# Matmuls without readers at three waits of TensorE in a kernel of attention and two layers

## The chip, the cores and the metric

The kernel runs on one core of one Trainium2 chip. The metric is the device time of one execution in microseconds (us), as a median of several executions. The engines are named as in the profile: PE is TensorE's matmul, PEld its weight load, DVE is VectorE, ACT ScalarE, POOL GpSimd, SP SyncE, which issues most DMAs.

## The reference

Attention over B=2 batches, H=8 heads, S=576 positions and head size 64 keeps the 32 largest scores of each row, takes the softmax over them and multiplies by the values. The result, 1152 tokens of 512, goes through two layers:

```python
scores = scale * np.matmul(q, k.transpose(0, 1, 3, 2))
kth = np.partition(scores, -32, axis=-1)[..., -32:-31]
attn = softmax(np.where(scores >= kth, scores, -1e9))
x = (attn @ v)                                    # to 1152 x 512
h = x @ w_in;  g = np.maximum(h, 0) + alpha * np.minimum(h, 0)
x = g @ w_out                                     # moe1: 512 -> 2048 -> 512
out = (x @ w_a) * (x @ w_b) @ w_out2              # moe2: 512 -> 1536 -> 512
```

## The kernel before

The tokens are cut into six groups of 128, 128, 256, 256, 256 and 128 (M1), numbered 0 to 5 in the code. Each group passes three kinds of work: attention, the first layer (moe1) and the second (moe2). Attention goes in 72 tiles of 128 query rows by 576 keys, numbered in the order in which they run. Tiles 16 to 31 belong to group 2, the third; tiles 32 to 35 are the first of group 3 and take the last 64 rows of two heads at a time; from tile 36 on the tiles belong to batch 1.

One tile goes through these steps. front() (L439 to L442): PE computes the scores into `ps`, a PSUM tile of two banks whose tag "S" has a single buffer, 288 columns in each bank, and ACT copies them to `s`. middle(): DVE takes the 8 largest four times (MAX8 on L450 and L459, MATCH_REPLACE8 on L457 between them); meanwhile ACT writes the exp of `s` into `ep` (L463), which takes the same single buffer of tag "S" as `ps`; DVE selects by the 32nd value and sums (L466), so it frees the buffer; POOL divides by the sum (L473). back(): in batch 0 PE transposes the tile (L500, L502) and ACT copies it out (L501, L503); in batch 1 the tile is split into two fp16 parts and transposed by a DMA that SP issues (L495). av(): PE multiplies by the values (L534 in batch 0 with 20 matmuls, L529 in batch 1 with 27 and one more), ACT (L542) and DVE (L543) write the two fp16 parts of the result, `xT`. The scores of the next tile are asked for while the present one is scanned.

moe1 of a group: for each of 16 blocks of features, l1 computes `h` on PE in 12 matmuls (L614, 256 columns in groups 2 to 4), ACT scales it to `r` (L649), DVE forms `gt` (L650), ACT and POOL split it in two parts `gp` (L604, L605); l2 accumulates `y` three blocks later (L626, 512 columns). finish() scales `y` by a power of two from its squares (ACT L684, DVE L114 to L116), splits it (ACT L694, DVE L695), transposes it on PE into `tp` (L699, PSUM tag "T" with two buffers, which the transposes of attention and av's result share), and ACT copies it to `xT` (L700). moe2 then computes `ha` and `hb` (L614, 12 matmuls each), ACT L753 and DVE L754 multiply them, and `o` accumulates (L626). Beside all this the weights are converted in the background (ACT L253 and L264, ACT L254 and L265, POOL L255 and L266), w2 through DRAM.

The order of the stages is ORDER: the two layers of groups 0 to 3 in turn, then moe1 of 4 and 5, then moe2 of 4 and 5. Three tracks (attention, conversion, layers) are interleaved by a planner's clock when the program is written; the framework then schedules the instructions of all engines by its own timeline, with priorities, and so sets the order on each engine. Each engine runs its queue in that order.

## Time and profile before

| | us |
|---|---|
| median of 3 runs | 723.14 |
| lowest, highest | 721.69, 1243.16 |
| the profiled execution | 723.9 |
| its span, first to last instruction | 722.0 |
| mean granted clock of TensorE, as a share of full speed | 0.942 |
| busy PE | 620.3 (86%) |
| busy DVE | 576.0 (80%) |
| busy ACT | 472.5 (65%) |
| busy POOL | 429.5 (59%) |

The prediction's sum is made against the profiled execution, and is then moved by its difference from the median. The busy shares are means over very different stretches; the rows below are taken from single ones.

### The profile page before, as it was taken

How to read it: one execution, taken by the hardware profiler on the slowest of the kernel's cores; microseconds unless marked ns; L12 is line 12 of the kernel's file. 1: busy time of each engine (PE TensorE's matmuls, PEld its weight loads, DVE VectorE, ACT ScalarE, POOL GpSimd, SP SyncE). 2: the span in 40 equal slices, each digit the busy share in tenths (PEclk: the TensorE clock that was granted, in tenths of full speed). 3: DMA queues.
4: the chain of work that ended last, by engine and by line, in shares of the span. 5: the costliest groups of instructions: out<-in, count | busy, mean ns of one | idle time of the engine just before them, and what ended most of it. 6: DMA issues, size and time to landing. Idle time of an engine off the chain costs nothing.

```text
span 722.0 us, 14587 instructions
## 1 busy us (share of the span) xinstructions
PE 620.3 (86%) x4950; PEld 459.4 (64%) x4950; DVE 576.0 (80%) x1462; ACT 472.5 (65%) x967; POOL 429.5 (59%) x608
## 2 busy tenths in 40 slices
PE   2555758899989898879977999998899989899997
PEld 1334546678666676656735777765677767677775
DVE  4999899779999998799788889999899989322121
ACT  5957988797699896789778544556455545543232
POOL 5856788888456675679787655555355545321111
PEclk9998678999999998979996999999799999999999
DMA  6966998995440041222547544422355531102233
GB/s 183 336 201 197 308 310 272 311 340 154 137 117 25 15 113 37 78 75 80 151 138 202 155 106 109 108 56 58 47 104 125 102 64 34 34 2 59 63 128 103
DMA packets 98490, 94.55 MB, mean 131 GB/s; under 512 B 50416, under 2 KB 72688, under 8 KB 98416
## 3 DMA queue, kind: packets, MB, share of 16 engines
q1 hardware_dynamic: 97104, 91.26, 44.5%
q10 hardware_dynamic: 1312, 2.36, 1.1%
q8 instruction: 39, 0.64, 0.4%
q14 instruction: 35, 0.29, 0.1%
HBM read 74.33 MB, written 8.65 MB: 115 GB/s over the span
## 4 chain that ended last, share of the span: by engine, by line
PE 43%; DVE 22%; ACT 9%; DMA 8%; issue 6%; POOL 4%; SPq 1%; POOLq 0%; DVEq 0%; ACTq 0%
DVE wk L457 6%; PE h L614 6%; DVE m L459 6%; PE y L626 5%; PE hb L614 5%; PE ha L614 5%; PE o L626 5%; DVE e L466 3%; PE ps L439 3%; DMA pt<-e 3%; PE hb L618 2%; PE ha L618 2%; DMA w2s<-w_st 2%; DVE m L450 2%; PE o L534 2%
## 5 line engine op out<-in xcount | busy, mean ns | idle before, releaser
L459 DVE MAX8 m<-wk 128x8 f32<-128x576 f32 x216 | 163.0, 754 | 2.5
L605 POOL TENSOR_TENSOR gp<-gt,gp 128x256 f16<-128x256 f32 (+1 forms) x112 | 68.3, 612 | 119.0 <-ACT gp L604 108.4
L457 DVE MATCH_REPLACE8 wk<-m,wk 128x576 f32<-128x576 f32 x144 | 106.8, 742 | 0.0
L614 PE MATMUL h<-xT,wi_sb 128*128 128x256 f16 (+1 forms) x960 | 98.3, 251 | 2.1 <-DVE gp_n L663 0.7
L614 PEld LDWEIGHTS <-wi_sb 128*128 128x128 f16 x960 | 79.1, 98 | 23.7 <-issue 7.3
L604 ACT ACTIVATE gp<-gt 128x256 f16<-128x256 f32 (+1 forms) x112 | 43.3, 387 | 68.0 <-DVE gt L754 44.7
L626 PE MATMUL y<-wo_sb,gp 128*128 128x512 f16 x336 | 84.9, 385 | 3.1 <-ACT gp L604 2.0
L626 PEld LDWEIGHTS <-gp 128*128 128x128 f16 x588 | 54.8, 98 | 51.0 <-ACT gp L604 3.8
L439 PE MATMUL ps<-ks,qh 128*128 128x288 f32 x160 | 49.9, 395 | 40.5 <-DVE e L466 31.4
L473 POOL TENSOR_SCALAR e<-e,sm 128x576 f32<-128x576 f32 x72 | 55.2, 767 | 37.7 <-DVE sm L471 36.6
L450 DVE MAX8 m<-s 128x8 f32<-128x576 f32 x72 | 54.2, 753 | 26.3 <-ACT s L442 25.9
L754 DVE SCALAR_TENSOR_TENSOR gt<-hb,wb_inv,r 128x256 f32<-128x256 f32 (+1 forms) x48 | 21.4, 446 | 60.6 <-PE hb L614 60.3
L614 PE MATMUL ha<-xT,wa_sb 128*128 128x256 f16 (+1 forms) x576 | 66.3, 265 | 1.5 <-ACT xT L700 1.3
L614 PE MATMUL hb<-xT,wb_sb 128*128 128x256 f16 (+1 forms) x576 | 63.9, 260 | 0.7 <-DVE gt L754 0.7
L626 PE MATMUL o<-w2s,gp 128*128 128x512 f16 x252 | 63.8, 379 | 0.4 <-ACT gp L604 0.2
L439 PEld LDWEIGHTS ps<-ks,qh 128*128 128x128 f32 x160 | 29.7, 217 | 53.8 <-DVE e L466 28.6
L614 PEld LDWEIGHTS <-wa_sb 128*128 128x128 f16 x576 | 51.6, 100 | 15.8 <-issue 1.9
L466 DVE SCALAR_TENSOR_TENSOR e<-s,m,ep 128x576 f32<-128x576 f32 x72 | 58.1, 806 | 3.0 <-PE t L502 0.7
L442 ACT ACTIVATE s<-ps 128x576 f32<-128x576 f32 x72 | 46.6, 647 | 15.4 <-PE ps L439 14.9
L614 PEld LDWEIGHTS <-wb_sb 128*128 128x128 f16 x576 | 50.7, 98 | 7.7 <-issue 0.7
L195 ACT ACTIVATE rlo<-raw 128x512 int16<-128x512 uint32 x68 | 54.2, 797 | 2.0 <-DMA raw<-in_wi_dram 1.7
L463 ACT ACTIVATE ep<-s,nb 128x576 f32<-128x576 f32 x72 | 54.0, 750 | 1.8 <-DVE e L466 0.6
(204 smaller groups left out, 1435.1 us busy)
## 6 DMA issues: line engine op xcount, KB each, us to landing
w2s<-w_pr SPq DMA_DIRECT2D x48, 256.0 KB, 2.8
w2s<-w_st SPq DMA_DIRECT2D x36, 256.0 KB, 2.8
raw<-in_wi_dram SPq DMA_DIRECT2D x16, 512.0 KB, 6.9
raw<-in_wo_dram SPq DMA_DIRECT2D x16, 512.0 KB, 6.8
raw<-in_wa_dram SPq DMA_DIRECT2D x12, 512.0 KB, 5.4
raw<-in_wb_dram SPq DMA_DIRECT2D x12, 512.0 KB, 5.0
raw<-in_w_dram SPq DMA_DIRECT2D x12, 512.0 KB, 5.0
kr<-in_kT_dram SPq DMA_DIRECT2D x32, 144.0 KB, 2.9
```

Of the source, the lines that this page charges most:

```text
L195: nc.scalar.activation(r.bitcast(I16).rearrange("p (n t) -> p n t", t=2)[:, :, 0], lo, AF.Copy, scale=2.0 ** -29)
L439: nc.tensor.matmul(ps[:, f, 0:HALF], q[:, h % 2, :], ks[h][:, f * HALF:(f + 1) * HALF], start=i == 0, stop=i == len(mm) - 1)
L442: nc.scalar.activation(s.rearrange("p (a n) -> p a n", a=2), ps[:, :, 0:HALF], AF.Copy)
L450: nc.vector.max(m8[:, 0:8], s)
L457: nc.vector.match_replace(out=wk, in_to_replace=m8[:, 8 * r - 8:8 * r], in_values=src, imm_value=NEG)
L459: nc.vector.max(m8[:, 8 * r:8 * r + 8], wk)
L463: nc.scalar.activation(ep, w2(s), AF.Exp, bias=nb, scale=0.125)
L466: nc.vector.scalar_tensor_tensor(w2(e), w2(s), m8[:, 31:32], ep, op0=ALU.is_ge, op1=ALU.mult, accum_out=sm[:, 0:1])
L473: nc.gpsimd.tensor_scalar(e, e, sm[:, 1:2], 1.0, op0=ALU.mult, op1=ALU.mult)
L605: nc.gpsimd.tensor_sub(l[:, 0:n], t[:, 0:n], h[:, 0:n])
L614: nc.tensor.matmul(dst[:, 0:n], w[a][:, c * P:(c + 1) * P], x[:, b, c, 0:n], start=k == 0, stop=k == 11)
L626: nc.tensor.matmul(dst, act[b][:, s], w[a], start=i == 0 and k == 0, stop=i == last and k == 2)
```

## The change

The tiles of attention get their number as `i`. Two tables say where matmuls are added whose results nobody reads:

- WARM_S in front(): for tiles 31, 32 and 33, after ACT's copy of the scores, 14 matmuls of 224 columns into the columns 288 to 511 of the two banks of `ps`, from operands that the scores used.
- WARM in l1: for groups 2 and 3, after the last of the 16 blocks, 16 and 8 matmuls of 256 columns into the second half of `h`.
- WARM in finish(): for groups 2 and 3, before the transposes of token tile 0 and 1, 8 and 6 matmuls of 512 columns into `tp`, which the transposes then write over.

```diff
--- before.py
+++ after.py
@@ -65,6 +65,8 @@
 HPY = 0
 HPM = 100
 SB = 3
+WARM = {2: (16, 8, 6), 3: (8, 8, 6)}
+WARM_S = {31: 14, 32: 14, 33: 14}
 KBACK = 2
 KFRONT = 2
 SHIFT_ATT = 4.0
@@ -392,6 +394,8 @@
                         tiles.append(dict(g=g, b=b, t=t if kind == "T" else 4, hp=hp, hs=hs, n=n, col=cols_of[unit[0]], slot=slot,
                                           wide=len(unit) * P, pts=pts_of, lift=b == 1, last=slot == len(unit) - 1 and i == len(heads) - 1))
         gsize.append(col)
+    for i, tl in enumerate(tiles):
+        tl["i"] = i
 
     def fetch(tl):
         b, t, hp = tl["b"], tl["t"], tl["hp"]
@@ -440,6 +444,8 @@
                                  start=i == 0, stop=i == len(mm) - 1)
         s = sp.tile([P, S], F32, tag="s", name="s", bufs=SB)
         nc.scalar.activation(s.rearrange("p (a n) -> p a n", a=2), ps[:, :, 0:HALF], AF.Copy)
+        for i in range(WARM_S.get(tl["i"], 0)):
+            nc.tensor.matmul(ps[:, i % 2, HALF:512], qh[:, tl["hs"][0] % 2, :], ks[tl["hs"][0]][:, 0:512 - HALF], start=True, stop=True)
         return s
 
     def middle(tl, s):
@@ -649,6 +655,10 @@
                     nc.scalar.activation(r1[:, 0:n], h[:, 0:n], AF.Copy, scale=pre_sig[:, fc:fc + 1])
                     nc.vector.scalar_tensor_tensor(gt[:, 0:n], h[:, 0:n], pre_alp[:, fc:fc + 1], r1[:, 0:n], op0=ALU.mult, op1=ALU.max)
                     gts[fc] = act_split(gt, n)
+                if fc == NF1 - 1 and g in WARM:
+                    for i in range(WARM[g][0]):
+                        nc.tensor.matmul(h[:, 256:256 + n], halves("wi", fc)[0][:, 0:P], xT[:, 0, 0, 0:n], start=True, stop=True)
+                if s2:
                     return
                 r1, r2 = (sized("r1", 2, n, s2), sized("r2", 2, n, s2))
                 nc.scalar.activation(r1[:, 0:n], h[:, 0:n], AF.Relu, scale=pos[:, fc // 2:fc // 2 + 1] if s1 else 2.0)
@@ -693,7 +703,11 @@
                 yh, yl = yb[:, 0:DM], yb[:, DM:2 * DM]
                 nc.scalar.activation(yh, ys[t], AF.Copy, scale=sq[:, 1:2])
                 nc.vector.scalar_tensor_tensor(yl, ys[t], sq[:, 1:2], yh, op0=ALU.mult, op1=ALU.subtract)
-                tp = psum("tp", "T").bitcast(F16).rearrange("p (a c n) -> p a c n", a=2, c=4)
+                tp = psum("tp", "T")
+                if g in WARM:
+                    for i in range(WARM[g][1 + min(t, 1)]):
+                        nc.tensor.matmul(tp, gts[NF1 - 1][0][:, t * P:(t + 1) * P], halves("wo", NF1 - 1)[0], start=True, stop=True)
+                tp = tp.bitcast(F16).rearrange("p (a c n) -> p a c n", a=2, c=4)
                 for i, y in enumerate((yh, yl)):
                     for c in range(4):
                         nc.tensor.transpose(tp[:, i, c, :], y[:, c * P:(c + 1) * P], ident16)
```

The numbers of lines grow by 2 to 14 with the change (L439 becomes L443, L529 L535, L534 L540, L543 L549, L626 L632, L699 L713). PE gets 94 matmuls and 52 weight loads more; the other engines have the same instructions as before in another order.

PE at the end of group 2, before. The lines L500 and L502 are transposes of attention tiles, L439 scores (ks_116 is of tile 32, ks_149 of tile 33), L534 the product with the values, L629 moe2 of group 1:

```order
L629 MATMUL o_3083<-w2s,gp_n 128x512 x2
L500 MATMUL t_3755<-ident,e 128x128 x4
L502 MATMUL t_3756<-ident,e 128x128
L439 MATMUL ps<-ks_116,qh_3615 128x288 x2
L439 MATMUL ps<-ks_116,ql_3616 128x288 x2
L500 MATMUL t_3803<-ident,e 128x128 x4
L502 MATMUL t_3804<-ident,e 128x128
L439 MATMUL ps<-ks_149,qh_3693 128x288 x2
L534 MATMUL o<-pt,v_3629 64x256 x10
```

The same place after the change; L448 are the added matmuls of front(), 14 of them for each of the three tiles (qh_3447 is of tile 31):

```order
L448 MATMUL ps<-ks_422,qh_3447 128x224 x9
L635 MATMUL o_3083<-w2s,gp_n 128x512
L448 MATMUL ps<-ks_422,qh_3447 128x224 x2
L506 MATMUL t_3755<-ident,e 128x128 x4
L508 MATMUL t_3756<-ident,e 128x128
L443 MATMUL ps<-ks_116,qh_3615 128x288 x2
L443 MATMUL ps<-ks_116,ql_3616 128x288 x2
L506 MATMUL t_3817<-ident,e 128x128 x4
L508 MATMUL t_3818<-ident,e 128x128
L448 MATMUL ps<-ks_116,qh_3615 128x224 x14
L443 MATMUL ps<-ks_149,qh_3693 128x288 x2
L540 MATMUL o<-pt,v_3629 64x256 x10
```

The set of tile 31 stands among the last matmuls of `o`, ahead of the transposes; the set of tile 32 stands behind the next transposes and ahead of the scores of tile 33.

PE at the change from moe1 to moe2 in group 2, before. y_3997 and y_3998 are the two token tiles of `y`, ks_4632 belongs to tile 42, vp_2913 and vp_3493 are values, and `tp` the transposes of finish(). Repeated rows are left out:

```order
L439 MATMUL ps<-ks_4632,qh_4644 128x288 x2
L439 MATMUL ps<-ks_4632,ql_4645 128x288 x2
L439 MATMUL ps<-ks_4638,qh_4644 128x288 x2
L439 MATMUL ps<-ks_4638,ql_4645 128x288 x2
L626 LDWEIGHTS gp
L529 LDWEIGHTS vp_2913
L529 MATMUL o<-pt,vp_2913 64x128
L699 LDWEIGHTS yb
L699 MATMUL tp<-ident_72,yb 128x128
```

The same place after; L660 are the added matmuls of l1 (16), L709 those of finish() (8 here). Tile 42's keys are now ks_4674, and `y` is y_4039 and y_4040:

```order
L660 MATMUL h<-xT_2844,wi_sb 128x256
L632 MATMUL y_4039<-wo_sb,gp 128x512
L709 LDWEIGHTS gp
L709 MATMUL tp<-wo_sb,gp 128x512
L535 LDWEIGHTS vp_2913
L535 MATMUL o<-pt,vp_2913 64x128
L632 MATMUL y_4040<-wo_sb,gp 128x512
L443 MATMUL ps<-ks_4674,qh_4686 128x288 x2
L443 MATMUL ps<-ks_4674,ql_4687 128x288 x2
L443 MATMUL ps<-ks_4680,qh_4686 128x288 x2
L535 MATMUL o<-pt,vp_3493 64x64
```

The scores of tile 42 stood ahead of the last `y` and of the product with vp_2913; now they stand behind both, and two sets of added matmuls stand ahead.

DVE at the same place, before; m_5130 are the maxima of tile 42, m_4974 those of tile 41, L543 the second part of the product with vp_2913:

```order
L457 MATCH_REPLACE wk<-m_4974,wk 128x576
L450 MAX m_5130<-s 128x8
L114 TENSOR_SCALAR e_4948<-ysq 128x1
L115 TENSOR_SCALAR ysq<-e_4948 128x1
L114 TENSOR_SCALAR e_5061<-ysq 128x1
L459 MAX m_4974<-wk 128x8
L543 SCALAR_TENSOR_TENSOR xT_3972<-o,xT_3972 128x128
L457 MATCH_REPLACE wk<-m_5130,s 128x576
```

DVE there after; m_5202 are the maxima of tile 42 now, m_5040 those of tile 41, L549 the product's second part, L705 the split of `y`:

```order
L463 MATCH_REPLACE wk<-m_5040,wk 128x576
L549 SCALAR_TENSOR_TENSOR xT_4014<-o,xT_4014 128x128
L116 TENSOR_SCALAR e_5006<-ysq 128x1
L465 MAX m_5040<-wk 128x8
L117 TENSOR_SCALAR ysq<-e_5006 128x1
L116 TENSOR_SCALAR e_5127<-ysq 128x1
L807 TENSOR_SCALAR u<-ysq 128x1
L456 MAX m_5202<-s 128x8
L705 SCALAR_TENSOR_TENSOR yb<-y_4039,ysq,yb 128x512
```

The product's second part stood behind the first scan of tile 42 and the last of tile 41; now it stands ahead of both.

## Rows read from the trace of the kernel before

**Rows 1.** The page's part 2: the span in 40 slices, in tenths.

```profile
DVE  4999899779999998799788889999899989322121
...
PEclk9998678999999998979996999999799999999999
```

**Rows 2.** Stretches: length, busy PE, PEld, DVE, ACT, POOL (count), granted clock, DMA share, GB/s.

```profile
307.30:317.60 10.30, 7.31 (x31) 5.04 (x33) 10.13 (x26) 7.96 (x14) 9.02 (x13) 0.51 0.23 66
375.80:382.30 6.50, 5.07 (x16) 2.79 (x15) 5.63 (x14) 2.71 (x6) 6.36 (x14) 0.50 0.62 151
386.00:396.20 10.20, 7.13 (x62) 5.56 (x63) 8.51 (x21) 9.47 (x18) 8.41 (x11) 0.50 0.89 230
505.30:515.70 10.40, 7.65 (x54) 6.11 (x54) 9.22 (x25) 4.94 (x8) 3.09 (x5) 0.51 0.22 41
420.00:500.00 80.00, 80.00 (x646) 56.90 (x643) 75.33 (x179) 42.74 (x88) 42.71 (x70) 1.00 0.39 89
...
623.00:722.00 99.00, 93.64 (x940) 70.63 (x934) 21.22 (x53) 33.74 (x88) 20.02 (x40) 0.99 0.21 65
```

**Rows 3.** The chain of waits that ends last: start, length, what.

```profile
283.02 2.31 PE o L534 x20
...
322.52 1.33 PE ps L439 x8
...
379.05 2.26 PE ps L439 x8
...
619.10 3.18 DMA pt<-e
622.33 0.94 PE o L529 x27
...
671.40 1.29 PE o L626 x6
672.70 1.31 PE ha L614 x12
```

**Rows 4.** Timeline, all engines, 300 to 322 us; idle time before, and releaser, in brackets.

```profile
304.50 0.76 DVE L450 MAX8 m<-s 128x8 f32<-128x576 f32 x1 [1.08 <-ACT s L442]
...
304.90 0.66 PE L500 MATMUL t<-ident,e 128*128 128x128 f32 x4 [2.33 <-POOL e L473]
...
305.34 0.73 ACT L463 ACTIVATE ep<-s,nb 128x576 f32<-128x576 f32 x1
...
306.91 0.81 DVE L466 SCALAR_TENSOR_TENSOR e<-s,m,ep 128x576 f32<-128x576 f32 x1
...
307.79 0.85 PE L439 MATMUL ps<-ks,qh 128*128 128x288 f32 x2 [2.12 <-DVE e L466]
...
313.91 4.20 PE L534 MATMUL o<-pt,v 128*64 128x256 f32 x20 [2.35 <-ACT pt L501]
...
320.12 0.76 DVE L450 MAX8 m<-s 128x8 f32<-128x576 f32 x1 [0.93 <-ACT s L442]
```

**Rows 5.** Timeline, all engines, 372 to 396 us.

```profile
373.80 0.60 PE L626 MATMUL y<-wo_sb,gp 128*128 128x512 f16 x2 [2.02 <-ACT gp L604]
...
382.03 0.76 DVE L450 MAX8 m<-s 128x8 f32<-128x576 f32 x1 [0.74 <-ACT s L442]
...
382.77 0.97 PE L529 MATMUL o<-pt,vp 128*64 128x128 f16 x27
...
393.40 2.72 PE L614 MATMUL ha<-xT,wa_sb 128*128 128x256 f16 x12 [0.18 <-ACT xT L700]
...
395.21 0.76 DVE L450 MAX8 m<-s 128x8 f32<-128x576 f32 x1 [1.65 <-ACT s L442]
```

**Rows 6.** Timeline, all engines, 503 to 520 us.

```profile
506.55 3.15 PE L529 MATMUL o<-pt,vp 128*64 128x256 f16 x27 [1.58 <-DMA pt<-e]
...
512.75 2.72 PE L614 MATMUL ha<-xT,wa_sb 128*128 128x256 f16 x12 [1.11 <-ACT xT L700]
...
517.05 0.48 DVE L754 SCALAR_TENSOR_TENSOR gt<-hb,wb_inv,r 128x256 f32<-128x256 f32 x1 [1.64 <-PE hb L614]
```

## The prediction

> **What bounds the kernel now.** I read the two lines of the page's 40 slices first [rows 1]. A slice is 18 us. The granted clock of TensorE drops early on (slices 4 to 7), which the change doesn't touch, and then to 7, 6 and 7 in slices 18, 22 and 29, which are the places of the change. VectorE (DVE) is at 7 tenths or more in each slice until the 34th, and at 3 or less behind it. The busy time by stretch then says what the drops are [rows 2]. In four stretches the granted clock is 0.50 or 0.51, which is the lower of the engine's two levels, 1.2 GHz. TensorE (PE) worked 7.31 + 5.07 + 7.13 + 7.65 = 27.2 us in them, and at 2.4 GHz it would have needed half, so 13.6 us is the most that the clock could give back there. Between 420 and 500 us PE is busy in all 80.00 us and DVE in 75.33, so there the two are close to each other as bounds, with 4.67 us of idle DVE.
>
> The chain of waits [rows 3] gives the end: the last attention tile's transpose by DMA (619.10, 3.18 us), its product with the values at 622.33, and behind it only layer work. That tail is PE's: 93.64 of 99.00 us at a clock of 0.99 [rows 2]. The changed order has as many PE rows behind that last product as the old one, so a gain counts only if it brings the last attention tile forward. Attention goes through DVE, which takes its scans strictly in its own order. So I price the change by the DVE idle time that it removes or adds, and treat PE time as the bound only in a rival.
>
> The three places are seen in the timelines. At the third group's tiles [rows 4], PE stands idle 2.33 us before the transposes at 304.90 and 2.12 us before the scores at 307.79, and from there the clock is low. At the first change of layers [rows 5], it idles 2.02 us before the y matmuls at 373.80, then works at the low clock. At the second [rows 6], the product at 506.55 waits 1.58 us for a DMA and is followed by the hidden-layer matmuls ha at the low clock, 2.72 us for twelve.
>
> **The change, part by part.** It removes no instruction. It adds 94 matmuls without readers: 42 of 224 columns in front(), 24 of 256 columns in l1, 28 of 512 columns in finish. The other engines get no work, but the scheduler orders all engines anew.
>
> *Price of the added matmuls.* Eight score matmuls of 288 columns take 1.33 us at the high clock and 2.26 at the low one [rows 3]. Scaled to 224 columns that is 0.129 and 0.22 each, so a set of 14 is an estimated 1.8 us (3.1 if cold). Twelve matmuls of 256 columns take 1.31 us and six of 512 take 1.29 [rows 3], so 0.109 and 0.215 each. In all 42 x 0.129 + 24 x 0.109 + 28 x 0.215 = 14.0 us on PE. The idle PE time within the four cold stretches alone is 37.4 - 27.2 = 10.2 us [rows 2], and more lies just ahead of each, so I cost these matmuls nothing as work. They cost where somebody waits behind them.
>
> *Place A, tiles 31 to 33.* The scores' PSUM slot has one buffer, and the exp output ep takes the same slot next, so the exp waits for the added matmuls. For tile 31 they stand ahead of the DVE gap of 1.08 us at 304.50 [rows 4]; a set of 1.8 us costs between 0 and 0.7, and I take 0. For tile 32 they stand behind the transposes that wait for GpSimd (304.90, 0.66 us long), so they run from about 305.6 to 307.4. The exp that began at 305.34 and took 0.73 then ends near 308.1, and the DVE select that began at 306.91 moves by 1.2 us. For tile 33 I expect no further delay. Against that, the scores at 307.79 should be warm and 0.9 us shorter (2.26 - 1.33), and the product of twenty at 313.91 should take 2.31 us as at 283.02 [rows 3] instead of 4.20. DVE's only idle time behind these is 0.93 us at 320.12 [rows 4], so no more than that comes back. Sum: +1.2 - 0.9 = +0.3, with ends at -0.9 and +3.2 (the set for tile 32 cold, 1.3 more, tile 31's 0.7, and nothing given back).
>
> The Trainium skill has a rule that bears on this place: the page "PSUM — Partial Sum Buffer", section "PSUM bank collisions raise a hardware error", says that two engines must be kept apart by bank, even where their columns are disjoint. By that rule "free columns" are not free: the added matmuls need the copy out of both banks to be over and hold the next user back, which makes place A +0.3; if columns were independent the exp could start as before and A would be -0.9, giving 719.3. The order shows the wait; no run here shows a collision.
>
> *Place B, first change of layers.* The added matmuls wait here for the last activation of l1 and for a slot. The order moves two other things. The scores of one tile now stand behind the product with vp_2913 on PE, and on DVE the xT row of that product stands ahead of a tile's last scans. Before, the product ran at 382.77 and took 0.97 us [rows 5]; with the copy by ScalarE behind it, xT can run near 383.9. DVE arrives there near 381.3 (382.03 less its gap of 0.74). So it waits 2.6 instead of 0.74 us, +1.8. The scores warm give back 0.9 us of the gap of 1.65 at 395.21. Net +0.9, with ends at -2.4 (both gaps gone, no new one) and +5.0 (one transpose of 3.18 more). ha at 393.40 would shrink from 2.72 to 1.31 [rows 3, 5], but that is PE time, which counts in the next term.
>
> *The stretch from 400 to 500.* PE arrives up to 1.4 us earlier by ha and about as much by hb, and DVE has 4.67 us to fill [rows 2]. The order also puts the score matmuls of most later tiles before some us of layer work that they followed. Ends: 0 and -4.7. Just ahead of it the chain runs through DMAs, not PE, so I take a third, -1.5.
>
> *Place C, second change of layers.* The product at 506.55 would halve from 3.15 us, ha and hb too. DVE was idle 1.18 us within the stretch [rows 2] and until 517.05 after it, 1.35 more. All of that should go: about -2.4. The cover is the 1.58 us of DMA wait ahead of the product; the 8 matmuls in h and 8 + 6 in tp are 0.9 + 3.0 us, which delay y, whose readers have time until the transposes after the product. Without cover +1.5 instead. Ends: -2.5 and +1.5.
>
> **Sum.** +0.3 + 0.9 - 1.5 - 2.4 = -2.7 us. The profiled execution took 723.9 us (span 722.0), 0.8 over the median of 723.14. So 721.2 in that execution's terms, and about 720.5 as a median. The ends add up to -10.5 and +9.7, so 713 to 733 if all fell on one side.
>
> **Rivals.**
> *PE bounds throughout.* For it: 80.00 of 80.00 us busy, and a PE queue in which every score stands behind layer work. Then all 27.2 us of cold work count half, -13.6, and the time is 709.5. Against it: in the stretch at 307 DVE is busy 10.13 of 10.30 us while PE has 2.99 idle [rows 2], so there at least the clock is not what ends the stretch.
> The Trainium skill's page "TensorE: Matmul & The Clock Gate", Part 1, says that the ramp costs under 1% of a typical kernel's span; by that no more than 7.2 us could come back, and this rival would end at 716 instead. The trace does not agree with it as a bound: half of 27.2 us is 1.9% of 722.0, since the clock falls more than once.
>
> *Slower: DVE is held by what now stands ahead of it.* The mechanism is place B's and A's: DVE's queue is in order, and the moved xT row and the exps make it wait for a PE queue with cold added matmuls and a DMA transpose in it. If the clock is low when the added sets run, each of the three exps waits 3.1 us, 9.3, and if the transpose comes one later, 3.18 us are added: 12.5 us in all, and the time is 735.6. Half of it is 729. It decides if the added sets run after the fall of the clock, not before. For it: the set for tile 32 stands behind a wait of 2.33 us [rows 4]. Against it: the transposes that end that wait still run at the high clock, four in 0.66 us.
>
> *The change doesn't do what it says.* The added matmuls wait themselves: for ScalarE's copy, for DVE's gt, for a slot in the tag T. If the idle time before them is what lowers the clock, it falls all the same. Then no cold work gets faster, place A and B cost about 2 to 3 us, and some of it is absorbed: 724.5. For it: the gap of 2.02 us at 373.80 [rows 5] stands before the first added matmul of place B can run.
>
> **How the numbers follow.** The forecast gets 0.50; with the distances of its terms from their ends put together as a root of squares (4.7 down, 6.5 up) its own range is 716 to 727. PE as the bound 0.14, DVE held 0.17, no effect on the clock 0.19. The likeliest case gives 720.5. The range goes from 710 to 731: it leaves out the lower half of the PE case and the upper half of the DVE case, and some of each case's own spread, about 0.18. A change of 2%, 14.5 us, is about what a measurement of this kernel can tell from none. Faster than 708.7 needs more than the whole PE case: 0.07. Slower than 737.6 needs the DVE case in full and something more: 0.05. The rest, 0.88, is within 2%.
>
> **What would show it.** Right, if in the changed kernel's profile the granted clock stays near 1.0 through the stretches at 307, 376, 386 and 505, the product of twenty near 314 takes 2.3 us, ha after each change of layers takes 1.3, and the last attention product comes 2 to 4 us before 622.33, with the tail still 99 us. Place A is right if DVE's select of tile 32 waits for its exp, about 1.2 us. Place B is right if the xT row after the product with vp_2913 shows a DVE wait of more than 2 us. The forecast is wrong if the last attention product moves by over 8 us in either direction: forward, if PE was the bound from 400 on; back, if DVE's waits for scores, exps or xT have grown. It is wrong in its ground if the clock still falls at these places, or if the time changes in the tail, which should not move.

## The result, and the profile after

The changed kernel takes 731.52 us (median of four, 727.5 to 733.8); the kernel before took 722.99 beside it. The ratio is 1.0121, with a 95% interval from 1.0083 to 1.0159: slower by 8.5 us, just outside the range of 710 to 731. A second set of nine executions gave 730.27 and 1.0082 [1.0052, 1.0113].

The page's slices, to be read against [rows 1]:

```profile
DVE  4899899789899995888888689999999999222121
...
PEclk9976669999999998989998999999999999999999
```

The clock in slices 18, 22 and 29 reads 8, 8 and 9 now, where it read 7, 6 and 7. The mean clock of these slices rises, as the change meant it to, and the kernel is slower all the same. Its profiled execution took 731.0 us, its span 729.2, with a mean granted clock of 0.94, as before. The stretches of the kernel after say where the clock went (columns as in [rows 2]):

```profile
303.50:312.40 8.90, 3.74 (x28) 3.30 (x28) 6.77 (x16) 6.17 (x12) 5.78 (x9) 0.88 0.22 58
312.40:318.00 5.60, 5.60 (x29) 5.29 (x29) 3.10 (x8) 4.49 (x7) 4.86 (x8) 0.59 0.15 38
...
391.00:402.00 11.00, 7.29 (x62) 4.57 (x63) 10.76 (x28) 9.13 (x17) 8.34 (x13) 0.69 0.85 182
...
512.00:530.00 18.00, 15.31 (x113) 11.35 (x111) 16.99 (x42) 9.73 (x18) 8.41 (x14) 0.91 0.28 45
```

The low stretch has moved and not vanished: it lies at 312 to 318 us now (0.59) and again at 391 to 402 (0.69). At group 3's change of layers (512 to 530) it is nearly gone, 0.91 over 18 us against the 0.51 of [rows 2] over 10.4 us.

**How two profiles are compared here.** All engines' orders are the same in all kernels until tile 28, yet DVE's select of that tile starts between 273.2 and 282.4 us in the profiles; the spread is 1.8 us at the first tile's select and 9.0 at tile 16's, and no run shows its cause. So each select's start is taken from that of tile 28 in the same profile, and compared with the same difference in the kernel before. For tile 32 in the changed kernel: (319.19 - 277.18) - (314.79 - 279.21) = +6.4 us. Tiles are counted from 0. The rows of the kernel before that this needs, and tile 30's:

```profile
279.21 0.81 DVE L466 SCALAR_TENSOR_TENSOR e<-s,m,ep 128x576 f32<-128x576 f32 x1
...
297.36 0.63 ACT L442 ACTIVATE s<-ps 128x576 f32<-128x576 f32 x1
...
298.93 0.73 ACT L463 ACTIVATE ep<-s,nb 128x576 f32<-128x576 f32 x1
...
300.28 0.80 DVE L466 SCALAR_TENSOR_TENSOR e<-s,m,ep 128x576 f32<-128x576 f32 x1
...
301.01 0.60 ACT L796 ACTIVATE ob<-o 128x512 f32<-128x512 f32 x1 [0.37 <-PE o L629]
...
314.79 0.80 DVE L466 SCALAR_TENSOR_TENSOR e<-s,m,ep 128x576 f32<-128x576 f32 x1
```

The scores of tile 31 are copied by 297.99, tile 30's exp, which takes the slot next, starts at 298.93, and the copy of the layer's output (ob) comes behind it on ScalarE. Place A in the changed kernel, timeline of PE, DVE and ACT together:

```profile
277.18 0.81 DVE L472 SCALAR_TENSOR_TENSOR e<-s,m,ep 128x576 f32<-128x576 f32 x1
...
295.96 0.65 ACT L446 ACTIVATE s<-ps 128x576 f32<-128x576 f32 x1 [0.25 <-PE ps L443]
...
297.66 1.24 PE L448 MATMUL ps<-ks,qh 128*128 128x224 f32 x9
...
300.29 0.89 PE L448 MATMUL ps<-ks,qh 128*128 128x224 f32 x3
...
300.89 0.60 ACT L810 ACTIVATE ob<-o 128x512 f32<-128x512 f32 x1 [2.15 <-PE o L635]
...
302.71 0.73 ACT L469 ACTIVATE ep<-s,nb 128x576 f32<-128x576 f32 x1
...
303.55 0.81 DVE L472 SCALAR_TENSOR_TENSOR e<-s,m,ep 128x576 f32<-128x576 f32 x1 [0.44 <-ACT ep L469]
...
306.60 0.76 DVE L456 MAX8 m<-s 128x8 f32<-128x576 f32 x1 [1.84 <-ACT s L446]
...
311.43 0.80 DVE L472 SCALAR_TENSOR_TENSOR e<-s,m,ep 128x576 f32<-128x576 f32 x1
...
312.39 0.82 PE L443 MATMUL ps<-ks,qh 128*128 128x288 f32 x2 [4.02 <-DVE e L472]
...
317.96 2.38 PE L540 MATMUL o<-pt,v 128*64 128x256 f32 x20
...
319.19 0.82 DVE L472 SCALAR_TENSOR_TENSOR e<-s,m,ep 128x576 f32<-128x576 f32 x1 [0.39 <-issue]
```

The set of tile 31 waits for the copy that ends at 296.61, starts at 297.66 behind layer matmuls, and ends at 301.18, because the order has cut it in three with `o` matmuls between: 3.5 us instead of 1.8. Then ScalarE does the output copy, which waited 2.15 us for these `o` matmuls, a conversion and the next queries, and only then the exp, at 302.71. A set holds back the exp of the tile before: the prediction names the exp by the tile of the set, here it is named by its own. DVE selects at 303.55. From the end of the copy to the exp it was 0.94 us before and is 6.1 now. Counted from tile 28's select, the exp starts 5.8 us later than before; the set's end, ahead of which it could not start, accounts for 4.3 of them, and what ScalarE does in between for the last 1.5. PE then stands idle 4.02 us before the scores at 312.39, the clock falls there, and the scores run cold again.

Place B and what follows it:

```profile
383.86 0.97 PE L535 MATMUL o<-pt,vp 128*64 128x128 f16 x27
...
385.25 0.28 DVE L549 SCALAR_TENSOR_TENSOR xT<-o,xT 128x128 f16<-128x128 f32 x1
...
390.92 0.47 PE L535 MATMUL o<-pt,vp 128*64 128x64 f16 x17 [4.06 <-DMA pt<-e]
...
401.69 1.47 PE L620 MATMUL ha<-xT,wa_sb 128*128 128x256 f16 x12 [0.72 <-ACT xT L714]
...
410.81 0.61 PE L443 MATMUL ps<-ks,qh 128*128 128x288 f32 x2
...
411.53 0.43 PE L443 MATMUL ps<-ks,qh 128*128 128x288 f32 x2
...
416.48 0.48 DVE L768 SCALAR_TENSOR_TENSOR gt<-hb,wb_inv,r 128x256 f32<-128x256 f32 x1 [2.61 <-PE hb L620]
...
418.17 0.53 PE L443 MATMUL ps<-ks,ql 128*128 128x288 f32 x2
...
418.75 0.23 DVE L549 SCALAR_TENSOR_TENSOR xT<-o,xT 128x64 f16<-128x64 f32 x1 [1.79 <-ACT xT L548]
...
420.20 0.81 DVE L472 SCALAR_TENSOR_TENSOR e<-s,m,ep 128x576 f32<-128x576 f32 x1
```

The eight scores of tile 45 are cut in two by the order: six at 410.81 to 412.0, the last two at 418.17, with 6 us of layer work between. DVE waits 2.61 and 1.79 us behind that in its queue, and the select of tile 44 slips to 420.20. The product with vp_2913 (383.86, 0.97 us) doesn't wait, and its xT row at 385.25 has no idle time before it; the one that waits 4.06 us for its DMA is the next, with vp_3493. The first ha of moe2, at 401.69, takes 1.47 us here; in a second profile of the same kernel (e10) it takes 2.72. Place C, and the begin of the tail (PE alone):

```profile
510.46 1.69 PE L535 MATMUL o<-pt,vp 128*64 128x256 f16 x27
...
519.41 1.47 PE L620 MATMUL ha<-xT,wa_sb 128*128 128x256 f16 x12 [0.42 <-ACT xT L714]
...
628.18 0.40 PE L713 MATMUL tp<-ident,yb 128*128 128x128 f16 x4 [0.60 <-ACT yb L704]
...
631.19 2.72 PE L620 MATMUL h<-xT,wi_sb 128*128 128x128 f16 x24 [0.85 <-DVE gt L656]
```

The product of 27 takes 1.69 us instead of the 3.15 of [rows 6], ha 1.47 instead of 2.72. In the tail PE waits 0.60 and 0.85 us and runs 24 short matmuls at the low clock, 2.72 us. In the second profile (e10) PE waits 0.85 us there too, but the same 24 run at the high clock:

```profile
630.43 1.50 PE L620 MATMUL h<-xT,wi_sb 128*128 128x128 f16 x24 [0.85 <-DVE gt L656]
```

### The profile page after: what moved, and what is told of

Read it like the earlier page. It is cut to its first block, busy times and chain, and to the rows that moved or that the text cites. A ratio compares the mean times of both kernels' runs of the same rounds, so it can differ in the third digit from the quotient of the medians.

```text
span 729.2 us, 14780 instructions
## 1 busy us (share of the span) xinstructions
PE 630.7 (86%) x5044; PEld 467.5 (64%) x5044; DVE 571.1 (78%) x1462; ACT 470.4 (65%) x967; POOL 430.7 (59%) x608
## 5 line engine op out<-in xcount | busy, mean ns | idle before, releaser
L620 PE MATMUL h<-xT,wi_sb 128*128 128x256 f16 (+1 forms) x960 | 102.1, 257 | 2.3 <-DVE gt L656 1.1
L620 PEld LDWEIGHTS <-wi_sb 128*128 128x128 f16 x960 | 81.3, 100 | 27.1 <-issue 10.0
L443 PE MATMUL ps<-ks,qh 128*128 128x288 f32 x160 | 50.0, 394 | 43.4 <-DVE e L472 34.1
L632 PE MATMUL y<-wo_sb,gp 128*128 128x512 f16 x336 | 85.1, 382 | 0.1
L632 PEld LDWEIGHTS <-gp 128*128 128x128 f16 x588 | 55.3, 98 | 45.6 <-issue 1.5
L443 PEld LDWEIGHTS ps<-ks,qh 128*128 128x128 f32 x160 | 29.6, 212 | 55.9 <-DVE e L472 23.4
L632 PE MATMUL o<-w2s,gp 128*128 128x512 f16 x252 | 64.6, 379 | 0.9 <-DMA w2s<-w_pr 0.5
L620 PE MATMUL ha<-xT,wa_sb 128*128 128x256 f16 (+1 forms) x576 | 63.8, 259 | 1.1 <-ACT xT L714 1.1
L463 DVE MATCH_REPLACE8 wk<-m,s 128x576 f32<-128x576 f32 x72 | 53.4, 742 | 0.0
```

The costliest lines, as they stand in the source:

```text
L443: nc.tensor.matmul(ps[:, f, 0:HALF], q[:, h % 2, :], ks[h][:, f * HALF:(f + 1) * HALF], start=i == 0, stop=i == len(mm) - 1)
L463: nc.vector.match_replace(out=wk, in_to_replace=m8[:, 8 * r - 8:8 * r], in_values=src, imm_value=NEG)
L620: nc.tensor.matmul(dst[:, 0:n], w[a][:, c * P:(c + 1) * P], x[:, b, c, 0:n], start=k == 0, stop=k == 11)
L632: nc.tensor.matmul(dst, act[b][:, s], w[a], start=i == 0 and k == 0, stop=i == last and k == 2)
```

## The experiments

All times are medians beside executions of the kernel before on the same chip, with the ratio and its interval. The table gives the shift of DVE's select (us, later is +) as worked out above, and in the last column that of the end of the span.

| kernel | 30 | 32 | 43 | 44 | 49 | 57 | 58 | 61 | 71 | end |
|---|---|---|---|---|---|---|---|---|---|---|
| changed kernel | +5.3 | +6.4 | +4.6 | +9.7 | +6.0 | +6.1 | +4.8 | +7.3 | +5.9 | +9.2 |
| e10, the same again | +3.9 | +4.6 | +4.2 | +9.5 | +5.9 | +5.9 | +3.9 | +6.7 | +4.5 | +6.1 |
| e1, front() alone | +3.9 | +4.8 | +5.2 | +8.9 | +5.1 | +7.1 | +7.0 | +7.9 | +10.7 | +11.3 |
| e2, layers alone | +0.4 | +0.3 | -0.4 | +7.6 | +2.5 | +3.4 | +1.4 | +2.4 | +4.2 | +4.8 |
| e11, the same again | +0.7 | +0.8 | +2.1 | +9.8 | +4.7 | +5.6 | +3.6 | +4.6 | +6.9 | +7.5 |
| e3, one each | +0.2 | -2.5 | +0.3 | +3.7 | -0.4 | -0.3 | -0.3 | +0.6 | +4.0 | +4.6 |
| e4, front() in its own bank | +0.6 | -0.5 | +1.9 | +5.7 | +1.6 | +1.6 | +2.0 | +2.2 | -0.3 | +1.1 |
| e5, front() with priority | +1.1 | +3.7 | +12.1 | +15.5 | +10.5 | +11.0 | +8.9 | +9.5 | +9.0 | +9.6 |
| e6, tile 31's set | +4.0 | +0.7 | +3.0 | +6.6 | +2.6 | +2.5 | +0.5 | +1.5 | +4.1 | +5.3 |
| e7, group 2 alone | -0.7 | -0.4 | +0.1 | +7.8 | +2.7 | +3.9 | +1.8 | +1.9 | -0.1 | +1.4 |
| e8, group 3 alone | -0.1 | +0.3 | +0.7 | +0.6 | +0.6 | +0.4 | -1.4 | -0.7 | +1.8 | +3.1 |
| e9, five each | +0.2 | +0.1 | -2.2 | +2.0 | -2.1 | -2.2 | -3.6 | -2.6 | -2.8 | -2.2 |
| e12, whole, own bank | -0.6 | -1.7 | +2.1 | +0.3 | 0.0 | -0.3 | -2.2 | -1.5 | -2.7 | -2.7 |
| e14, the same again | +0.5 | -0.6 | +4.1 | +2.1 | +1.8 | +1.5 | -0.4 | +0.3 | -0.6 | -0.6 |
| e13, layers, scores together | 0.0 | +0.3 | +5.1 | +4.9 | +4.2 | +3.8 | +2.0 | +2.7 | +2.1 | +3.7 |
| e15, whole, slot held | +4.4 | +7.2 | +5.8 | +11.1 | +7.4 | +7.4 | +6.5 | +7.5 | +10.1 | +10.7 |

Each row is one execution; the three pairs of the same kernel (changed and e10, e2 and e11, e12 and e14) differ by up to 3 us, so a single entry is good to a few us, while a jump that comes again is the order's. In all three pairs the execution that reached tile 28 later has the smaller shift at the end, which suggests that part of a late start is made up behind it. The last column is not the time either: e3 has +4.6 there and the median of the kernel before, e4 has +1.1 and a median 4.9 us above that of the kernel before. The table places a delay and does not price a kernel. The changed kernel's line jumps three times: at tile 30, at tile 44, and at the end.

The jump at tile 44 is not the layers' sets alone. e1, e3, e4, e5, e6 and e9, which have none of them, jump by 3.4 to 4.2 us there, and by tile 49 all of it is given back; in e3, e4, e6 and e9 the scores of tile 45 are cut in two with over 6 us between, as here in e9:

```profile
404.60 0.29 PE L443 MATMUL ps<-ks,qh 128*128 128x288 f32 x1
...
411.12 0.40 PE L443 MATMUL ps<-ks,qh 128*128 128x288 f32 x1
```

e3 and e9 take the time of the kernel before all the same. With the sets of group 2 (changed, e10, e2, e11, e7, e15) 1.5 to 2.9 us of the jump are left at tile 49.

The theories at the start: Q, that the sets in front() hold the exp through PSUM and ScalarE's queue and so delay DVE; L, that the sets at the changes of layers, or what the order does behind them, cost the time.

**e1, e2: one half each.**

```diff
-WARM = {2: (16, 8, 6), 3: (8, 8, 6)}
+WARM = {}                                  # e1
-WARM_S = {31: 14, 32: 14, 33: 14}
+WARM_S = {}                                # e2
```

> Only the 3 x 14 matmuls of front() for tiles 31 to 33; none in l1 and finish(). Theory Q (ScalarE's queue): the added sets hold the exp's PSUM slot and the query buffers, so that tile 31's exp stands on ScalarE behind the output copy, a weight conversion and tile 33's queries; DVE's selects of tiles 31 and 32 come about 5 us later than in the kernel before (as in the changed kernel, where from tile 29 on +5.8 us were added), and most of it stays: 726 to 731 us. Theory L (the sets at the changes of layers and the order behind them are the price): within 1.5 us of the kernel before, 721.5 to 724.5.

> Only the added matmuls of l1 and finish(), for groups 2 and 3; none in front(). Theory Q: place A is as in the kernel before, and the rest is worth little either way: 720 to 725 us, DVE's select of tile 32 near 314.8. Theory L: most of the 8.8 us is here, 728 to 733.

Measured: e1 734.22 us, 1.0159 [1.0116, 1.0202]; e2 730.56 us, 1.011 [1.0068, 1.0152]. Each half alone costs: e1 lies above Q's range (726 to 731), and not in the one that L gave it; e2 lies in L's (728 to 733). The halves don't add: 11 and 8 us apart, 8.5 together. That speaks for orders that hit or miss, on top of a price per matmul.

**e3, e9: the length of the sets in front().** Both are without the sets of l1 and finish().

```diff
-WARM_S = {31: 14, 32: 14, 33: 14}
+WARM = {}                                  # both
+WARM_S = {31: 1, 32: 1, 33: 1}             # e3
+WARM_S = {31: 5, 32: 5, 33: 5}             # e9
```

> One matmul in place of 14 for each of tiles 31, 32 and 33, none in l1 and finish(): the waits that the added matmuls bring (for ScalarE's copy, for the exp's slot, on the query buffers) stay, their length goes. If the length of the sets is the price (1.8 us each): 721.5 to 724. If the order on ScalarE that the mere dependence brings is the price: 726 to 730. In its order tile 31's exp stands behind the queries of tile 33 but ahead of the output copy, so a delay of DVE's select of tile 31 of 1 to 4 us is expected, and of tile 32 less.

> As e1, but 5 matmuls for each of tiles 31 to 33 in place of 14 (0.65 us a set in place of 1.8). One each took the kernel before's time (e3), 14 each 11.2 us more (e1). If the length counts beyond the slack of each hold (DVE idle 1.08 us at tile 31, 0.93 at tile 34): 722 to 726. If the loss starts as soon as the order on ScalarE changes: 728 to 732.

Measured: e3 722.87 us, 0.9998 [0.9968, 1.0027]; e9 723.59 us, 1.0004 [0.9965, 1.0042]. The dependence alone costs nothing, and the delay that e3 was expected to show at the select did not come (+0.2 at tile 30); the loss lies between 5 and 14 matmuls. At 5 the order keeps the first set in one piece ahead of the `o` matmuls and the exp ahead of the output copy, and tile 30's select is 0.2 us late; at 14 the order cuts the set in three. So length and order change together here.

**e4, e12, e14, e15: which hold.** In e4 and e12 the sets go into a bank of their own with the copied scores as both operands; in e15 they stay in the scores' banks and only the operands change, with 18 matmuls of 224 columns in place of 16 of 256. e4 has no sets in l1 and finish(), the others have all.

```diff
-        for i in range(WARM_S.get(tl["i"], 0)):
-            nc.tensor.matmul(ps[:, i % 2, HALF:512], qh[:, tl["hs"][0] % 2, :], ks[tl["hs"][0]][:, 0:512 - HALF], start=True, stop=True)
+        if tl["i"] in WARM_S:
+            wm = psum("wm")
+            sv = s.bitcast(BF16).rearrange("p (n t) -> p n t", t=2)[:, :, 1]
+            for i in range(WARM_S[tl["i"]]):                 # 16 each
+                nc.tensor.matmul(wm[:, 0:256], sv[:, 0:P], sv[:, 0:256], start=True, stop=True)
```

> The three sets of front() go into a bank of their own (tag H), 16 matmuls of 256 columns each with the copied scores as both operands, so that neither the exp's slot nor the query and key buffers wait for them; as much TensorE time (1.8 us each), none in l1 and finish(). Theory Q: without the hold the loss goes, 721 to 724.5 us, with the exp of tile 31 where it was on ScalarE. If the TensorE time in front of the transposes and scores is the price: 726 to 731. If the kept clock is worth anything it shows here: the product of twenty near 314 takes 2.3 instead of 4.2 us, worth at most the DVE gap of 0.9 behind it.

> The whole change, but with the sets of front() in a bank of their own and on their own operands, as in e4. If the hold on the exp's slot and on the query buffers makes the changed kernel slow, this is faster than it by 3 to 7 us: 724 to 728. If the order or the sets' time at the other places does: 729 to 733.

> The kernel of e12 once more (the whole change with the sets of front() in their own bank and on their own operands), which took 1.0 us less than the kernel before, with an interval from -4.5 to +0.7. If the kept clock is worth what place C's stretch shows (DVE 1.9 us earlier at tile 58): 720 to 723 and from tile 28's select to the end again 2 to 3 us under the kernel before. If e12 was chance: 723 to 726.

> The whole change with the sets of front() in the free columns of the scores' banks as before (18 of 224 columns each), but with the copied scores as both operands: the exp's PSUM slot is still held, the query and key buffers are not. If the slot is what costs at place A: tile 30's select 3 to 5 us late, 728 to 733. If the query buffers are (POOL's and ScalarE's work for the next queries waits for the sets): tile 30's select at most 1.5 us late, 722 to 727.

Measured: e4 727.96 us, 1.0064 [1.0036, 1.0093], more than Q had said and in the range of its rival, PE's time (726 to 731); e12 722.34 us, 0.9974 [0.9938, 1.001]; e14 again 722.34 us, 0.9974 [0.9945, 1.0004]; e15 729.08 us, 1.0088 [1.0046, 1.0131]. The same change, with no less work on PE (a warm set takes 1.99 us in e12 and 1.82 in the changed kernel), is 1.1 to 1.5% faster once neither is held (0.9974 against 1.0082 and 1.0121), and slow again with the slot alone. So the hold on the slot is enough for the loss; the query buffers alone were not run. What was expected of e14, 2 to 3 us under the kernel before from tile 28 to the end, came in e12's profile (-2.7) and not again (-0.6): a gain is not shown. e15's timeline shows the same queue as the changed kernel's:

```profile
293.07 1.05 PE L449 MATMUL ps<-s 128*128 128x224 bf16 x9
...
296.10 0.66 PE L449 MATMUL ps<-s 128*128 128x224 bf16 x5
296.30 0.60 ACT L811 ACTIVATE ob<-o 128x512 f32<-128x512 f32 x1 [2.21 <-PE o L636]
...
297.83 0.74 ACT L470 ACTIVATE ep<-s,nb 128x576 f32<-128x576 f32 x1
...
298.67 0.82 DVE L473 SCALAR_TENSOR_TENSOR e<-s,m,ep 128x576 f32<-128x576 f32 x1 [0.23 <-ACT ep L470]
```

The set is cut in pieces again, the output copy waits 2.21 us, and the exp comes behind it. In e12 the granted clock from 300 to 322 us is 0.92 (0.77 in the kernel before): it falls there too, behind a wait of 1.64 us at 312, so that the third set takes 2.81 us, but it is up again for the product of twenty. The scores of tile 45 stay together:

```profile
313.43 2.81 PE L451 MATMUL wm<-s 128*128 128x256 bf16 x16
...
317.04 2.38 PE L543 MATMUL o<-pt,v 128*64 128x256 f32 x20
...
410.52 0.51 PE L443 MATMUL ps<-ks,qh 128*128 128x288 f32 x2
...
411.39 0.43 PE L443 MATMUL ps<-ks,ql 128*128 128x288 f32 x2
```

The product of twenty takes 2.38 us, as in the changed kernel; tile 32's select is 1.7 us early in one profile and 0.6 in the other. What the clock gives at place A is no more than that. e4's 4.9 us over the kernel before are not explained by its profile, whose end is only 1.1 late: the profiled execution, 723.66 us, was the fastest of the ten.

**e5, e6: the first set.** e5 gives the matmuls of e1 and the exps of tiles 30 to 32 a high priority; e6 has the set of tile 31 alone.

```diff
+        with tc.high_priority(offset=HPM):
             for i in range(WARM_S.get(tl["i"], 0)):
...
+                if tl["i"] + 1 in WARM_S:
+                    with tc.high_priority(offset=HPM):
+                        nc.scalar.activation(ep, w2(s), AF.Exp, bias=nb, scale=0.125)
```

> As e1 (only the sets of front()), but these matmuls and the exps of tiles 30 to 32 get a high priority: the order then puts the set of tile 31 in one piece ahead of the last o matmuls, and tile 30's exp on ScalarE ahead of the output copy, the queries and a conversion. The matmuls and their time are the same. If the place on ScalarE was the price (in e1 tile 30's select came 4.6 us late, of which the set itself is 1.8): tile 30's select at most 2.5 us late and the time 725 to 729, 4 to 8 us under e1. If the sets' own TensorE time, in the way of the scores and transposes, is the price: as e1, 732 to 736.

> Only the 14 matmuls behind tile 31's scores, nothing else. If the first set brings the loss (tile 30's select 4.6 us late): 726 to 732. If the loss needs the cold wait that the second set makes (TensorE idle 4 us before 312 and cold scores after it): 721 to 725.

Measured: e5 732.53 us, 1.0134 [1.0053, 1.0214]; e6 729.62 us, 1.0112 [1.0041, 1.0182]. In e6 the first set alone brings the delay of tile 30 (+4.0), but at tile 32 only +0.7 of it is left, where the changed kernel, e10, e1 and e15, with all three sets at full length, have +4.6 to +7.2; what e6 loses in its median, 6.7 us, is not placed there. In e5 that delay is down to 1.1, as expected, but the time is not:

```profile
292.82 1.80 PE L449 MATMUL ps<-ks,qh 128*128 128x224 f32 x14
...
299.98 1.82 PE L449 MATMUL ps<-ks,qh 128*128 128x224 f32 x14
...
308.70 3.10 PE L449 MATMUL ps<-ks,qh 128*128 128x224 f32 x14
...
381.52 1.65 PE L540 MATMUL o<-pt,vp 128*64 128x128 f16 x27 [4.04 <-DMA pt<-e]
...
384.95 0.29 DVE L554 SCALAR_TENSOR_TENSOR xT<-o,xT 128x128 f16<-128x128 f32 x1 [1.99 <-ACT xT L553]
```

The third set now stands behind PE's wait and runs cold, 3.10 us where the first two take 1.8; and at place B the product waits 4.04 us for its DMA with the xT row behind it on DVE (1.99 us). From tile 40 to 43 the kernel loses another 5.6 us. e5 changes PE's order and ScalarE's together: they explain tile 30, and not the sum. The time lies in the range of e5's rival, PE's time in the way of scores and transposes (732 to 736); against that rival stand e12 and e14, with as much of it and no loss.

**e7, e8: the two groups apart.**

```diff
+WARM = {2: (16, 8, 6)}                     # e7
+WARM = {3: (8, 8, 6)}                      # e8
+WARM_S = {}
```

> Only the 16 + 8 + 6 matmuls at group 2's change of layers. e2 with both changes took 7.5 us more than the kernel before. If it is held scores and xT at group 2's change (place B): 727 to 732, with DVE's select of tile 44 some 5 us late. If it comes from group 3 or from the order of later stages: 721 to 725.

> Only the 8 + 8 + 6 matmuls at group 3's change of layers; all engines' orders are as in the kernel before until then (TensorE's first 3684 rows). My sum for this place was -2.4: 719 to 722.5, with the product of 27 near 506 in about 1.7 instead of 3.15 us. If the matmuls held the y rows or the order behind costs: 724 to 729.

Measured: e7 723.95 us, 1.0007 [0.996, 1.0054]; e8 724.19 us, 1.0016 [0.998, 1.0051]. In e8 place C does what was forecast:

```profile
506.58 1.69 PE L535 MATMUL o<-pt,vp 128*64 128x256 f16 x27 [1.46 <-DMA pt<-e]
...
513.49 1.49 PE L620 MATMUL ha<-xT,wa_sb 128*128 128x256 f16 x12
```

The product takes 1.69 us, and the select of tile 58 gains 1.8 us on that of tile 57; by tile 71 more than that is given back (+1.8), and the time is not the 719 to 722.5 us that were forecast. In e7 tile 44 slips by 7.7, and that is made up entirely. e7 also has the gain at tile 58, 2.1 us, without any set in group 3 and with the product cold:

```profile
511.04 2.94 PE L535 MATMUL o<-pt,vp 128*64 128x256 f16 x27 [0.23 <-DMA pt<-e]
```

DVE's order there has the scans of tile 58 ahead of the row of moe2 that waits 1.64 us for hb in [rows 6]. In e3, where DVE's order from tile 57 to 58 is that of e12, this row waits 1.88 us with the product at 2.73 us, and in e12, at 1.69, it hardly waits. So the clock can give this gain, and an order gives it without the clock.

**e10, e11: the changed kernel and e2 once more**, without an edit.

> The changed kernel once more, to see which places of its first profile come again. Its time from the select of tile 28 to the end was 9.2 us over the kernel before's: 5.9 until tile 71's select and 3.4 in the tail. If these are the order's doing: again +4.5 to +7.5 and +2.5 to +4. If the tail's part is chance (every other kernel had +0.6 to +1.5 there): +0.5 to +1.5. Time 729 to 733.

> The kernel of e2 (only the sets of l1 and finish()) once more: e2 took 7.5 us more, but each group's set alone 1.0 and 1.2 (e7, e8). If e2's number stands: 728 to 733. If four executions misjudged it: 722 to 727, and from tile 28's select to the end again about +5 over the kernel before's profile, or less.

Measured: e10 730.27 us, 1.0082 [1.0052, 1.0113]; e11 730.04 us, 1.008 [1.0042, 1.0118]. The places come again: tile 30 (+5.3 and +3.9), tile 44 (+9.7 and +9.5). The tail's part is 3.4 us in one and 1.7 in the other. e2's number stands.

**e13: the scores of tile 45 together.** e2 with the score matmuls of that tile at a high priority, so that only the split goes.

```diff
+TOP = 45
...
-        for i, (q, h) in enumerate(mm):
+        with tc.high_priority(offset=HPM if tl["i"] == TOP else 0):
+            for i, (q, h) in enumerate(mm):
```

> The kernel of e2 (only the sets of l1 and finish()), with the eight score matmuls of tile 45 at a high priority, so that the order keeps them together; in e2, e11 and the changed kernel 3 to 6 of them run, then 6.5 us of layer work, then the rest, and DVE waits. If that split is what e2 and e11 lose (6.7 to 7.5 us): the select of tile 44 no longer comes 7 to 10 us late, and the time is 722 to 726. If the split is made up again by tile 49 and the loss comes from the later order (tile 67): 727 to 731.

Measured: 727.7 us, 1.0077 [1.0043, 1.0111]. The jump at tile 44 is gone (+5.1 to +4.9), so the split made it; but another order loses 5 us between tiles 41 and 43, and the time stays. Which place makes the layers' sets cost 6.7 us alone, and nothing in e12, is not settled: e2 and e11 lose about 3 us more from tile 66 to 67 (+1.2 to +4.0, +3.4 to +6.6), e12 does not, and e13 loses elsewhere.

## Why the prediction was wrong

**Place A is the term that failed.** It was put at +0.3 us with ends at -0.9 and +3.2, and is +6.4 at tile 32's select (4.6 in e10). The step was "For tile 31 they stand ahead of the DVE gap of 1.08 us at 304.50 [rows 4]; a set of 1.8 us costs between 0 and 0.7, and I take 0". It cost 5.3 us (3.9 in e10) at tile 30's select. The mechanism, an exp that waits for the set, was the right one; the size took the set as 1.8 us in one piece and the exp as free to go behind it. The order shown ahead of the prediction has the set cut by `o` matmuls (9 and 2 of the 14 are seen there, the last 3 in the trace), and ScalarE's order, of which the prediction says nothing, has the exp behind the output copy. Tile 32's term, +1.2, came out as 1.25 (6.55 - 5.30, from tile 30 to 31), and that is luck. The select at 311.43 does not wait for its exp, which was to be the sign of place A; 0.76 us of the 1.25 is DVE's longer wait at 306.60 (1.84 us against 1.08 before), for scores that tile 30's late select had held. By e6 the sets of tiles 32 and 33 cost more than their term: without them the delay falls to +0.7 by tile 32, with them it stays. The -0.9 for the clock came with the product at 2.38 us, but e4 and e12 show that it gives DVE little, and in the changed kernel the scores before it were cold again.

**Place B** was put at +0.9 by a longer wait of the xT row. In the changed kernel that wait isn't there, and DVE even gains between tiles 39 and 43 (from +7.2 to +4.6; +5.5 to +4.2 in e10). What came instead, the split of tile 45's scores, I had not seen: +5.2, of which 3.7 come back by tile 49. In e5 the xT wait did appear. e9 has the same split and no loss by tile 49. The stretch after it, -1.5, gave nothing beyond that recovery: the shift is +6.0 at tile 49 and +6.1 at tile 57.

**Place C**, -2.4, came in sign: tile 58 gains 1.2 us on tile 57 (2.0 in e10, 1.8 in e8, 1.9 in e12 and e14), and the product ran warm. That the warm product is the reason is not shown, since e7 has the gain with the cold one, and of e4 and e6, both with the product at 1.69 us and ha cold at 2.72, only e6 has it. And it is lost again by tile 61, +2.5. There a transpose takes 5.14 us in the chain of waits that ends last, where that of [rows 3] took 3.18, and DVE waits 0.58 us behind it; the rest is rows that now stand ahead of the select, and 0.9 us comes back at tile 62:

```profile
536.30 5.14 DMA pt<-e
...
543.62 0.42 DVE L549 SCALAR_TENSOR_TENSOR xT<-o,xT 128x256 f16<-128x256 f32 x1 [0.58 <-ACT xT L548]
```

**The tail** was to stay and is 3.4 us longer, 1.7 in e10, where the other kernels have up to 1.6; PE's waits and the cold matmuls at 631.19 are the part that the rows show. In e10 the same waits stand ahead of warm matmuls (1.50 us instead of 2.72), which makes 1.2 of the 1.7 us between the two tails. The last attention product, which was to come 2 to 4 us earlier than at 622.33, comes at 626.61.

One reading of [rows 1] in the prediction is off: DVE is at 4 tenths in the first slice. No term uses it. And a change of 2% is not the least that can be told here: the interval of the result is 0.4% to either side.

**The rivals.** DVE held by what stands ahead of it, slower, 729 to 735.6, is the case that came, though not by its price, so that the time falls into its span by luck: the first set ran at the high clock, and the delay of tile 30 came by the order on PE and ScalarE. PE as the bound fell: e12 and e14 have the warm products and the warm ha, and their ratio of 0.9974 isn't clear of 1. That the clock would fall all the same is half true: it did so at place A, behind a new wait of 4.02 us at 312 us, and in e12, where nothing holds the exp, behind 1.64 us. The prediction put place A at +0.3 us with the two banks guarded as a whole, and at -0.9 with columns that are free for themselves. The Trainium skill's page "PSUM — Partial Sum Buffer" (section "PSUM bank collisions raise a hardware error") asks for the guard by bank and not by address. The wait is there in the trace, but the added matmuls of e15 lie both in the same banks and in the same single buffer of tag "S" as the exp, so these runs don't tell a hold by bank from a hold by buffer, and none shows a collision. The Trainium skill's page "TensorE: Matmul & The Clock Gate" (Part 1) puts the ramp under 1% of a typical kernel's span. What e12 and e14 got back, 0.26% with intervals that reach to 0.62% and 0.55%, agrees with that.

**A version without the loss.** e12 and e14 are the whole change without the hold: 722.34 us twice, both intervals just reaching 1. It is faster than the changed kernel by about 1% and not to be told from the kernel before. What stays open is how much of the difference is the hold itself and how much the other order that comes with it: e4, without the hold and without the layers' sets, is 4.9 us slower than the kernel before.

## What to carry to other kernels

A matmul without a reader is free only as work: it holds its PSUM buffer against the next user, and what that costs is read from where the set ends in PE's queue and from the queue of the engine that the user stands in, not from the length of the set alone. Such work can go into a bank that nobody waits for, on operands that nobody is to overwrite; that took the loss away in e12, and not in e4. Where a scheduler sets the order, compare a change with variants of the same work: here orders alone moved single tiles by 5 to 8 us, and the end by about 7.

## What the runs showed of the hardware

The low clock showed itself as expected, 1.82 us against 3.10 for the same set of 14 matmuls in one execution. Not expected was how little a kept clock is worth when another engine or a DMA ends the stretch: over its 12 executions e14 has a mean granted clock of 0.957, the kernel before beside it 0.941, and the times are the same within the interval. The time until tile 28 also varies by 9 us between executions with the same order (273.2 to 282.4 us), next to a spread of 717 to 730 us in whole times of the kernel before; it has to be taken out before two profiles are compared, and the three pairs above suggest that this takes out somewhat too much.
